# One written-out order exchanged for another: chunk-selecting attention followed by a gated feed-forward layer

## The chip, the cores and the metric

The kernel runs on one core of one Trainium2 chip. The core has five engines, each with its own queue of instructions: TensorE (PE in the profile) for matrix products, VectorE (DVE), ScalarE (ACT), GpSimd (POOL), and SyncE (SP), which issues most transfers; GpSimd issues those of the weights, because they are cast from fp32 to fp16 on the way. The metric is the time of one execution on the device in microseconds (us), lower is better.

## The reference

```
k_min, k_max = per chunk of 32 keys, over the chunk                # 24 chunks
ub     = sum_d max(q * k_min, q * k_max)        # bound of a query on each chunk
top    = the 6 chunks with the highest bound, among those not in the future
attn   = softmax(q k^T / 8, only keys of these chunks, only keys not later)
x      = (attn v), heads side by side           # 3072 tokens x 512
out    = (sigmoid(x w_gate) * (x w_val)) w_out  # 512 -> 1536 -> 512
```

There are 4 batches, 8 heads, 768 positions and 64 values per head. Inputs and output are fp32; inside the kernel most products run on fp16.

## The kernel before

The 24 blocks of 128 tokens are put into units of three, u0 to u7 (`units`). u0 holds the first blocks of batches 0 to 2, in which no chunk has to be chosen (`first`); the first block of batch 3 goes into u2. For each other unit the keys and queries are turned (`kT`, `qT` on TensorE for u1 and u2, `kt`, `qf` on VectorE for the rest), the bounds are multiplied out (`ub`), VectorE finds the sixth highest per query (`ubn`, `mx`, `ap`, `apt`), and the chosen mask becomes 64 more rows of the queries (`hqm`), so that one product gives masked scores (`sc`). ScalarE takes the exponential (`exp`), GpSimd cuts the diagonal blocks (`cm`), TensorE multiplies with v (`pv`), VectorE divides (`rz`, `x`), and the result is turned into `xT`: on TensorE for the first units (`xps`), by a transposing transfer on SyncE's queue from u3 on. The feed-forward layer of a unit is 12 pieces of `g` and `v` products, ScalarE's `tanh`, VectorE's `hg`, and the output: `o` products for u0 to u3, and for u4 to u7 a scheme with seven products in place of eight (`pair`, with sums `sw`, `tw`; `by7` does the same to most gate products of u5 to u7, with sums `ss`, `tt`). Thirty products without use, `fl_0` to `fl_29`, stand near the start.

No scheduler decides anything when the kernel is built. The string `ORDER` lists all 2010 operations by name, each with its engine (P, A, V, G, S for TensorE, ScalarE, VectorE, GpSimd, SyncE), and `SLOTS` gives each buffer its place in its pool, such as one of the eight PSUM banks. `Plan.order` checks that every operation stands behind those that it depends on, and the operations are emitted in that sequence; so each engine's queue is the list cut down to its letter, and an engine waits at the first operation that is not ready. Each operation also carries a cost and a mark `port`, which `Plan.order` does not read. The list was made elsewhere, by a search that used such costs and marks.

The lines that matter below: L569 `fl`, L575 `ident16` (the fp16 identity, a cast of the fp32 one), L588 to L596 the weight transfers (`wgp` is a quarter of the first third of the gate weights, `wg0` the other three quarters, `wg1`, `wg2`, `wv0` to `wv2`, `wo0` to `wo2` are thirds), L614 to L645 the other loads, L687 `kfT`/`qfT`, L724 `scf`, L731 `cmf`, L738 `pvf`, L434 GpSimd's copies (`hkp...` writes a constant pattern into the keys' mask rows, `vc` casts v), L1237 `g` and `v`, L989 `x`, L994 the transposing transfer.

Of the kernel before, what the change touches and what calls it, by code (L numbers as in the profile page):

```python
# [111 lines left out]
hq0_u1_0=A tanh_u0_2=A tanh_u0_1=A hg_u0_1=V ubn1_u1=V v_u0_3=P tanh_u0_3=A hg_u0_3=V ubm1_u1=V hg_u0_2=V tanh_u0_0=A hg_u0_0=V
hk0_u1_0=A hq1_u1_1=A sc_u1_0_2=P exp_u1_0_2=A sc_u1_1_2=P sc_u1_0_1=P sc_u1_0_0=P exp_u1_1_2=A sc_u1_1_0=P sc_u1_1_1=P
exp_u1_0_0=A exp_u1_0_1=A v_u0_7=P wo0=G hqm0_u1_2=G sc_u1_2_2=P exp_u1_2_2=A sc_u1_2_0=P exp_u1_2_0=A sc_u1_3_0=P sc_u1_3_2=P
exp_u1_3_2=A exp_u1_1_0=A sc_u1_3_1=P exp_u1_3_1=A exp_u1_3_0=A v16_0_3=G wo1=G v_u0_4=P sc_u1_2_1=P v_u0_6=P exp_u1_2_1=A
hk1_u1_0=G v16_0_2=G wo2=G mx1_u1=V ap1_u1=V apt1_u1=V hqm1_u1_0=V g_u0_5=P tanh_u0_5=A v_u0_5=P exp_u1_1_1=A hqm1_u1_2=A g_u0_6=P
tanh_u0_6=A g_u0_7=P tanh_u0_7=A hg_u0_7=V v16_0_1=G cm_u1_3=G pv_u1_3=P cm_u1_2=G hk1_u1_1=G g_u0_4=P tanh_u0_4=A hg_u0_4=V
vf1_3=G hq1_u1_2=G pv_u1_2=P sc_u1_5_1=P sc_u1_4_2=P sc_u1_4_1=P rz_u1_1=V x_u1_1=V exp_u1_4_1=A v_u0_9=P v_u0_10=P xps_u1_1=P
xT_u1_1=A exp_u1_4_2=A hg_u0_6=V hk1_u1_3=V hg_u0_5=V v_u0_8=P g_u0_10=P tanh_u0_10=A kcr1=V hg_u0_10=V g_u0_8=P tanh_u0_8=A
hg_u0_8=V sc_u1_5_2=P exp_u1_5_2=A g_u0_9=P tanh_u0_9=A hg_u0_9=V sc_u1_4_0=P exp_u1_4_0=A cm_u1_1=G pv_u1_1=P cm_u1_0=G qn_u2_2=G  # L120
sc_u1_5_0=P pv_u1_0=P exp_u1_5_0=A sc_u1_6_1=P exp_u1_6_1=A sc_u1_6_2=P exp_u1_6_2=A exp_u1_5_1=A sc_u1_7_2=P sc_u1_7_0=P
g_u0_11=P qT_u2_2=P sc_u1_7_1=P tanh_u0_11=A exp_u1_7_2=A exp_u1_7_0=A exp_u1_7_1=A kn_u2_1=V kT_u2_1=P rz_u1_0=V x_u1_0=V
xps_u1_0=P cm_u1_5=G pv_u1_5=P cm_u1_4=G pv_u1_4=P qf_u2_2=V q1_u2=S qn_u2_1=V qT_u2_1=P sc_u1_6_0=P kt_u2_1=A exp_u1_6_0=A
# [139 lines left out]
c22_u67=V out_u67_b1=S p4_u67=P p4z_u67=P c21_u67=V out_u67_1=S  # L263
# [1161 lines left out]
```

## Time and profile before

| | us |
|---|---|
| median of 3 runs | 282.62 |
| lowest, highest | 282.24, 283.18 |
| the profiled execution | 283.43 |
| its span, from the first to the last instruction | 281.7 |
| TensorE busy in the span | 268.8 |
| VectorE, ScalarE, GpSimd busy | 235.7, 180.5, 163.3 |

The span is what the views of the profile divide up; the profiled execution took 1.73 us more than its span. A busy TensorE need not be at its peak, since a product that starts late is still counted as running until its modelled end. The granted clock of TensorE was 1.00 over the whole span.

### The profile page before, as it was taken

Reading aid. Unit: us, or ns where it says so; the run is one execution under the profiler, and the core shown is the slowest. Engines: PE = TensorE matmul, PEld = TensorE weight load, DVE = VectorE, ACT = ScalarE, POOL = GpSimd, SP = SyncE. Lnnn points to the kernel's source line nnn. Section 1 sums busy time; section 2 is a strip of 40 time slices with the busy share of each in tenths; the row PEclk is TensorE's granted clock in tenths of the full one; section 3 lists DMA queues with packets and bytes.
Section 4 is the critical chain, followed back from the end, with each engine's and each line's share of the span. In section 5 each row is a group of like instructions: output and inputs, shape, how many; then the busy total and the mean of one; then the engine's idle time right before and its main releaser. Section 6 shows DMA issues by size and latency. Waiting matters only on the chain.

```text
span 281.7 us, 7507 instructions
## 1 busy us (share of the span) xinstructions
PE 268.8 (95%) x2806; PEld 188.9 (67%) x2806; DVE 235.7 (84%) x686; ACT 180.5 (64%) x386; POOL 163.3 (58%) x262
## 2 busy tenths in 40 slices
PE   5868989999999999999999999999999999999994
PEld 4645657667855665556687657776888688778683
DVE  4889846697998998886999987977889998888885
ACT  6377868669957943559689979987983422341520
POOL 5797743638464781823869956842685568063450
PEclk9999999999999999999999999999999999999999
DMA  6999999899999598977897230100310033000304
GB/s 161 246 254 204 205 216 209 180 192 210 178 214 182 131 195 162 199 142 141 164 154 111 63 89 16 40 0 2 73 74 2 1 81 126 2 1 2 150 2 150
DMA packets 131717, 34.70 MB, mean 123 GB/s; under 512 B 119776, under 2 KB 128736, under 8 KB 131680
## 3 DMA queue, kind: packets, MB, share of 16 engines
q1 hardware_dynamic: 126912, 29.50, 50.2%
q0 software_dynamic: 4768, 4.72, 10.0%
q8 instruction: 22, 0.36, 0.6%
q14 instruction: 15, 0.12, 0.1%
HBM read 30.67 MB, written 6.29 MB: 131 GB/s over the span
## 4 chain that ended last, share of the span: by engine, by line
PE 81%; DMA 9%; DVE 6%; issue 1%; SPq 1%; POOL 0%; DVEq 0%; POOLq 0%
PE v_u L1237 19%; PE g_u L1237 14%; PE o_u L1286 11%; PE sc_u L935 11%; PE p_u L1060 10%; PE pv_u L968 6%; DMA wg<-in_moe_w_gate_dram 6%; PE p_g_u L1169 5%; PE ube_u L874 3%; DMA kq_u<-in_k_dram 2%; DMA kf<-in_k_dram 1%; DVE x_u L989 1%; DVE tw L1031 1%; DVE ox L1077 1%; DVE hg_u L1258 1%
## 5 line engine op out<-in xcount | busy, mean ns | idle before, releaser
L946 ACT ACTIVATE att_u<-sc_u 128x512 f16<-128x512 f32 (+3 forms) x184 | 86.8, 571 | 8.6 <-PE sc_u L935 7.3
L1237 PE MATMUL v_u<-xT_u,wv 128*128 128x384 f16 x384 | 72.4, 326 | 0.1
L1258 DVE SCALAR_TENSOR_TENSOR hg_u<-gate_u,v_u 128x384 f16<-128x384 f16 x96 | 51.0, 544 | 18.6 <-ACT gate_u L1249 9.3
L1249 ACT ACTIVATE gate_u<-g_u 128x384 f16<-128x384 f32 x72 | 35.2, 498 | 42.2 <-PE g_u L1237 36.9
L1237 PE MATMUL g_u<-xT_u,wg 128*128 128x384 f16 x288 | 56.0, 326 | 2.1 <-DMA wg<-in_moe_w_gate_dram 1.5
L952 POOL TENSOR_SCALAR_AFFINE_SELECT att_u<-att_u 128x384 f16<-128x384 f16 (+1 forms) x56 | 28.5, 517 | 40.9 <-ACT att_u L946 39.8
L1237 PEld LDWEIGHTS <-wv 128*128 128x128 f16 x384 | 36.1, 98 | 20.5 <-DMA wv<-in_moe_w_val_dram 0.4
L1237 PEld LDWEIGHTS <-wg 128*128 128x128 f16 x288 | 26.7, 98 | 19.5 <-DMA wg<-in_moe_w_gate_dram 3.0
L1286 PE MATMUL o_u<-wo,hg_u 128*128 128x512 f16 x144 | 34.3, 379 | 0.0
L968 PE MATMUL pv_u<-v,att_u 128*128 128x65 f16 x640 | 26.3, 193 | 0.0
L968 PEld LDWEIGHTS <-att_u 128*128 128x128 f16 x640 | 24.2, 98 | 2.9 <-issue 0.6
L1206 DVE TENSOR_TENSOR f_g_u<-p_g_u,f_g_u 128x192 f32<-128x192 f32 (+1 forms) x72 | 24.9, 384 | 1.0 <-PE p_g_u L1169 0.4
L935 PE MATMUL sc_u<-hqe,hke 128*128 128x128 f16 (+2 forms) x220 | 25.4, 243 | 0.2
L935 PE MATMUL sc_u<-hqo,hko 128*128 128x128 f16 (+2 forms) x220 | 24.1, 243 | 0.1
L1286 PEld LDWEIGHTS <-hg_u 128*128 128x128 f16 x144 | 13.7, 98 | 13.4
L935 PEld LDWEIGHTS <-hke 128*128 128x128 f16 x220 | 16.5, 98 | 5.3 <-issue 0.8
L935 PEld LDWEIGHTS <-hko 128*128 128x128 f16 x220 | 16.4, 98 | 4.7 <-issue 0.4
L651 POOL CAST v<-v 128x512 f16<-128x512 f32 x23 | 14.5, 633 | 3.0 <-DMA v<-in_v_dram 2.5
L1249 ACT ACTIVATE gate_u<-f_g_u 128x384 f16<-128x384 f32 x24 | 11.9, 519 | 5.6 <-DVE hg_u L1258 2.9
L989 DVE TENSOR_TENSOR x_u<-pv_u,rz_u 128x384 f16<-128x384 f32 (+1 forms) x28 | 14.6, 524 | 0.9 <-DMA xT_u<-x_u 0.5
L897 DVE MAX8 mx_u<-ubn_u 128x8 f32<-128x8 f32 (+16 forms) x152 | 12.7, 159 | 0.3
L841 DVE STREAM_TRANSPOSE qf_u<-q 128x384 f32<-128x384 f32 (+2 forms) x28 | 11.7, 437 | 1.2 <-DMA q<-in_q_dram 1.2
(187 smaller groups left out, 507.9 us busy)
## 6 DMA issues: line engine op xcount, KB each, us to landing
v<-in_v_dram SPq DMA_DIRECT2D x23, 256.0 KB, 4.7
k<-in_k_dram SPq DMA_DIRECT2D x12, 384.0 KB, 5.5
q<-in_q_dram SPq DMA_DIRECT2D x12, 384.0 KB, 5.5
out_dram<-osb_u SPq DMA_DIRECT2D x12, 256.0 KB, 3.4
out_dram<-sw SPq DMA_DIRECT2D x8, 256.0 KB, 2.1
wv<-in_moe_w_val_dram POOLq DMA_DIRECT2D x3, 512.0 KB, 10.2
wo<-in_moe_w_out_dram POOLq DMA_DIRECT2D x3, 512.0 KB, 18.9
qf<-in_q_dram SPq DMA_DIRECT2D x8, 128.0 KB, 3.4
```

The source lines that it names most:

```text
L651: plan.add(f"v16_{b}_{ib}", {POOL: pool(H * D)}, lambda e: nc.gpsimd.tensor_copy(v16[b % 2][:, ib, :, 0:D], at(t)), reads=[t], writes=[("v ...
L935: nc.tensor.matmul(at(t)[:, o:o + 128 * m], hk[b % 2][e_][:, p, 128 * jb:128 * jb + 128], hq[u.side][e_][:, p, 128 * x:128 * (x + m)], sta ...
L946: plan.add(f"exp_{u.name}_{h}_{y}", {ACT: act(n)}, lambda e, t=t, att=att, b0=b0, n=n: nc.scalar.activation(at(att)[:, b0:b0 + n], at(t), ...
L952: nc.gpsimd.affine_select(out=dv, in_=dv, compare_op=ALU.is_ge, fill=0.0, base=0, pattern=[[0, u.m], [1, 128]], channel_multiplier=-1)
L968: nc.tensor.matmul(at(pv)[:, last, x, :], at(att)[:, c:c + 128], v16[b % 2][:, jb, h, :], start=(jb == 0), stop=(jb == ib))
L989: plan.add(f"x_{u.name}_{p}", {DVE: dve(u.t)}, lambda e: nc.vector.tensor_tensor(at(x_).rearrange("p a (e d) -> p e a d", e=2), at(pv)[:, ...
L1060: nc.tensor.matmul(at(to)[:, side], a(j)[:, i], b(j)[:, i], start=j == i == 0, stop=j == 2 and i == 1)
L1206: plan.add(f"{p}_{name}", {POOL: pool2(192 * n), DVE: dve(192 * n)} if slow else {DVE: dve(192 * n)}, lambda e: both(e).tensor_tensor(dst( ...
L1237: nc.tensor.matmul(at(t), w16[:, c, 128 * fb:128 * fb + 128], at(u.xt)[:, c, :], start=(c == 0), stop=(c == 3))
L1249: plan.add(f"tanh_{u.name}_{fb}", {ACT: act(T, not seven[0])}, lambda e, gv=gv, gate=gate: nc.scalar.activation(at(gate), gv(), AF.Tanh, s ...
L1258: plan.add(f"hg_{u.name}_{fb}", {DVE: dve(T)}, lambda e, vv=vv, gate=gate, hg=hg, fb=fb: nc.vector.scalar_tensor_tensor(at(hg)[:, fb % 2], ...
L1286: nc.tensor.matmul(at(o), at(hgs[fc // 2])[:, fc % 2, 128 * tb:128 * tb + 128], wo16[:, fc, lo:hi], start=(fc == 0), stop=(fc == NFB - 1))
```

## The change

`ORDER` and `SLOTS` are replaced as a whole. The operations are the same 2010, with the same sizes; 701 stand on TensorE and 128 on SyncE in both. Of the rest 118 stand on another engine than before: VectorE has 526 in place of 540, ScalarE 398 in place of 385, GpSimd 257 in place of 256. The only other changed line gives the cast `ident16` the mark `port`, which nothing in the kernel reads.

The diff, cut to the one line and the head of the list:

```diff
 ORDER = """
-ident=G ones16=V fl_4=P fl_2=P fl_8=P fl_3=P fl_1=P fl_0=P fl_29=P k2_u1=S kn_u1_2=A qf1_0=S kf1_0=S kf0_0=S fl_6=P fl_5=P epat0=V
-ap0=V epat=G hkp110=A hkp000=A hkp001=V kT_u1_2=P kcr0=V kt_u1_2=V hk0_u1_2=G vf1_1=G hkp011=V hkp010=G vf1_2=G hkp100=G kf1_2=S
-kf0_1=S kfT_0=P kxf1=V fl_17=P fl_10=P fl_7=P kx0_u1_2=V ident16=V kf16_0=V qf0_0=S qfT_0=P qf16_0=V qf1_1=S kf1_1=S kfT_1=P
...
+vf1_1=G k2_u1=S qf0_0=S ones16=V fl_4=P v10=G epat0=V epat=G ident=G hkp000=G ident16=V hkp110=V kf0_0=S kf1_0=S fl_13=P fl_0=P
+fl_10=P fl_6=P fl_7=P fl_1=P fl_2=P fl_11=P fl_5=P fl_3=P kn_u1_2=A fl_8=P kT_u1_2=P kt_u1_2=A fl_9=P ap0=V kcr0=V kfT_0=P kxf1=V
+kxf0=V fl_17=P fl_12=P qf1_0=S qfT_0=P qf0_1=S qf1_1=S qfT_1=P kf1_1=S kf16_0=V hk1_u1_2=A hkp011=A fl_18=P qf16_0=A qf16_1=A
...
     const("ident16", {DVE: (150, 230)}, lambda e: nc.vector.tensor_copy(ident16, ident32),
-          reads=["ident32"], writes=["ident16"], prio=-1.0)
+          reads=["ident32"], writes=["ident16"], prio=-1.0, port=True)
```

Cut down to single engines, the head of the list reads (B before, A after):

```
POOL B: ident epat hk0_u1_2 vf1_1 hkp010 vf1_2 hkp100 v10 v16_0_0 cmf_0_0 cmf_0_1 wgp cmf_1_0 vc_1 cmf_1_1
        hkf0 wg0 wv0 cmf_2_0 vc_2 kn_u1_3 cmf_2_1 kn_u1_1 v11 wv1 wg1 hq0_u1_3 hk0_u1_3 hq1_u1_3 wv2 hk0_u1_1 wg2
POOL A: vf1_1 v10 epat ident hkp000 hkp010 hkp001 v16_0_0 cmf_0_0 cmf_0_1 hkp100 vf1_2 cmf_1_0 vc_1 cmf_1_1
        wg0 cmf_2_0 wgp wv0 cmf_2_1 qn_u1_0 wv1 qn_u1_2 wg1 qm_u1_3 wv2 kcr_f hkf1 hkp101 wg2
DVE  B: ones16 epat0 ap0 hkp001 kcr0 kt_u1_2 hkp011 kxf1 kx0_u1_2 ident16 kf16_0 qf16_0 kf16_1 hq0 ap1 qf16_1
DVE  A: ones16 epat0 ident16 hkp110 ap0 kcr0 kxf1 kxf0 kf16_0 kf16_1 rzf_0_0 xf_0_0 rzf_0_1 xf_0_1 qf16_2
ACT  B: kn_u1_2 hkp110 hkp000 expf_0_1 expf_0_0 expf_1_0 expf_1_1 hk1_u1_2 kf16_2 expf_2_1 expf_2_0
ACT  A: kn_u1_2 kt_u1_2 hk1_u1_2 hkp011 qf16_0 qf16_1 expf_0_0 expf_0_1 expf_1_1 expf_1_0 hkp111 kn_u1_0 kf16_2
SP   B: k2_u1 qf1_0 kf1_0 kf0_0 kf1_2 kf0_1 qf0_0 qf1_1 kf1_1 qf0_1 vf_0 qf0_2 qf1_2 kf0_2 vf_1 k0_u1 q3_u1 q2_u1
        vf_2 q1_u1 k3_u1 q0_u1 k1_u1 v_0_3 v_0_2 v_0_1 qf1_3 k0_u2 q2_u2 k1_u2 q1_u2 q3_u2 q0_u2 k2_u2 k3_u2 qf0_3
SP   A: k2_u1 qf0_0 kf0_0 kf1_0 qf1_0 qf0_1 qf1_1 kf1_1 vf_0 kf0_1 qf0_2 qf1_2 k0_u1 q0_u1 kf0_2 kf1_2 vf_1 q3_u1
        q1_u1 vf_2 k3_u1 q2_u1 k1_u1 v_0_3 v_0_2 v_0_1 q2_u2 q1_u2 k1_u2 k0_u2 q3_u2 q0_u2 k2_u2 k3_u2 qf1_3
```

On TensorE the same operations stand ahead of the first `g` product in both lists (all thirty `fl`, the turns of the first blocks and of u1). Between that product and the first one on the last third of the gate weights (`g_u0_10`) the new list has three operations more: `sc_u1_5_2`, `sc_u1_5_0` and `pv_u1_0`. Of the turns of batch 3's first block `kfT_3` now stands behind 133 operations of TensorE in place of 135, and `qfT_3` behind 134 in place of 132; `o2_u0_1` stood ahead of `kfT_3` and now follows it. In SyncE's queue `xT_u5_3`, which completes u5's input, stood behind `xT_u6_1`, `xT_u6_2` and `xT_u6_0`, and now stands behind the first two of them. Further on the sequence of every stage is another, and ends in the same way: the seven products of the last output block, each behind its sums, with `p4_u67` and `out_u67_1` last.

More of the change, by code (lines that the diff above doesn't have):

```diff
@@ L352 @@
+gate_u7_6:1 v_u7_6:5 hg_u7_3:1 gate_u7_7:0 v_u7_7:1 p1_g4_u7:1 f0_g4_u7:2 f1_g4_u7:1 p26_g4_u7:1 p53_g4_u7:6 p74_g4_u7:7
+gate_u7_8:1 v_u7_8:0 hg_u7_4:4 gate_u7_9:0 v_u7_9:5 g_u7_10:7 gate_u7_10:3 v_u7_10:3 hg_u7_5:6 g_u7_11:6 gate_u7_11:2 v_u7_11:4
+p1_u7:1 p26_u7:6 p5_u7:7 p3_u7:4 p7_u7:0 p4_u7:2 p1_u67:3 p26_u67:3 p5_u67:5 p3_u67:1 p7_u67:6 p4_u67:7
 """
```

495 lines of the change are left out of this document (246 added, 249 removed).

## The prediction

> **What bounds the kernel now.** I read the page first, then the chain of waits in order of time, then what each engine waited for, then the first 45 us engine by engine.
>
> ```profile
> span 281.7 us, 7507 instructions
> PE 268.8 (95%) x2806; PEld 188.9 (67%) x2806; DVE 235.7 (84%) x686; ACT 180.5 (64%) x386; POOL 163.3 (58%) x262
> PE   5868989999999999999999999999999999999994
> DMA  6999999899999598977897230100310033000304
> PE 81%; DMA 9%; DVE 6%; issue 1%; SPq 1%; POOL 0%; DVEq 0%; POOLq 0%
> ```
>
> TensorE bounds it: dense from the third slice (7 us each) to the last. The transfers are as full over the first eight slices, so until some 57 us the data's arrival sets a floor of its own. The chain says where TensorE did not set the pace.
>
> ```profile
> 5.81 1.10 PE kfT L687 x4
> 13.20 6.11 DMA kq_u<-in_k_dram
> 27.00 15.51 DMA wg<-in_moe_w_gate_dram
> 42.57 1.47 PE g_u L1237 x8
> 176.17 0.56 DVE x_u L989
> 176.73 0.95 DVE mx_u L897 x12
> 178.32 0.87 issue
> 180.01 0.57 DVE x_u L989
> 186.91 0.77 DVE tw L1031
> 189.93 0.57 DVE x_u L989
> 277.85 0.70 DVE ox L1077
> ```
>
> The last third of the gate weights, issued at 27.00, held TensorE until 42.57. Between 43 and 277 us the longer pieces that are not TensorE's sum to 0.56 + 0.95 + 0.87 + 0.57 + 0.77 + 0.57 = 4.3 us; that is about all that any order could still win there. The end is one VectorE pass and a store.
>
> ```profile
> PE pvf L738 <- POOL vh L434: 1.9, 2, 1.2
> PE g_u L1237 <- DMA wg<-in_moe_w_gate_dram: 1.5, 2, 1.3
> PE g_u L1237 <- ACT xT_u L430: 0.6, 1, 0.6
> ```
>
> These columns are us in total, times, and the longest. All lie in the first 45 us. What happens there, engine by engine:
>
> ```profile
> 1.07 0.29 POOL masks.py:199 TENSOR_SCALAR_AFFINE_SELECT ident<-ident 128x128 f32<-128x128 f32 x1
> 4.00 0.55 DVE L432 COPY hke<-epat 64x1536 f16<-64x1536 f16 x1 [1.74 <-POOL epat L544]
> 5.34 0.54 DVE L432 COPY hko<-epat 64x1536 f16<-64x1536 f16 x1
> 5.57 0.67 POOL L434 COPY hke<-kt_u 64x384 f16<-64x384 f16 x1 [1.60 <-DVE kt_u L432]
> 7.82 1.46 POOL L434 COPY hke<-epat 64x1536 f16<-64x1536 f16 x1
> 8.00 1.36 DVE L575 CAST ident<-ident 128x128 f16<-128x128 f32 x1
> 9.29 0.68 DVE L432 CAST kf<-kfT 128x512 f16<-128x512 f32 x1
> 10.61 0.40 PE L724 MATMUL scf<-qf,kf 64*128 64x128 f16 x8 [0.76 <-DVE qf L432]
> 13.38 0.79 POOL L588 DMA_DIRECT2D wg<-in_moe_w_gate_dram  x1
> 16.46 0.80 POOL L590 DMA_DIRECT2D wg<-in_moe_w_gate_dram  x1
> 23.65 0.32 PE L1237 MATMUL g_u<-xT_u,wg 128*128 128x384 f16 x1 [0.59 <-ACT xT_u L430]
> 24.23 1.31 PE L1237 MATMUL g_u<-xT_u,wg 128*128 128x384 f16 x7 [0.26 <-DMA wg<-in_moe_w_gate_dram]
> 37.15 0.43 PE L968 MATMUL pv_u<-v,att_u 128*128 128x65 f16 x9
> 37.43 0.81 PE L1237 MATMUL g_u<-xT_u,wg 128*128 128x384 f16 x4
> 42.57 1.47 PE L1237 MATMUL g_u<-xT_u,wg 128*128 128x384 f16 x8 [1.27 <-DMA wg<-in_moe_w_gate_dram]
> 44.64 0.39 PE L935 MATMUL sc_u<-hqo,hko 128*128 128x128 f16 x4
> 44.86 0.44 PE L968 MATMUL pv_u<-v,att_u 128*128 128x65 f16 x9
> ```
>
> The cast at 8.00 ended at 9.36, just after GpSimd's copy (7.82 to 9.28): it sat behind that copy. The other way round at 5.34: VectorE's copy was first and took its 0.54, and GpSimd's of 5.57 took 0.67, with 0.31 of it beside the other. The first feed-forward product ran its first quarter at 23.65 and went on at 24.23, when the rest of its weights had come. The times to landing are on the page:
>
> ```profile
> wg<-in_moe_w_gate_dram POOLq DMA_DIRECT2D x1, 384.0 KB, 7.7
> wg<-in_moe_w_gate_dram POOLq DMA_DIRECT2D x1, 128.0 KB, 5.8
> ```
>
> So the small piece issued at 13.38 was there at 19.2, and the large one, issued at 16.46, at 24.2.
>
> **The change part by part.** The mark `port` emits nothing: 0. TensorE's work is the same, and its clock was full, so only the time in which it is held up can change.
>
> *Engines.* VectorE loses 14 operations, at 235.7/686 = 0.34 us some 4.8 us; ScalarE gains 13, at 180.5/386 = 0.47 us some 6.1; GpSimd gains one, 0.6. None bounds the whole (TensorE has 268.8), so I count 0, covered by TensorE's queue. Where that cover is thin, in the 176 to 190 us of the chain, VectorE's relief can give back up to the 4.3 us above, and ScalarE's load can cost as much.
>
> *The identity, the patterns and the first scores.* GpSimd now makes the pattern before the identity, and then three pattern copies (1.46 each) in a row. The cast moves from tenth to third on VectorE, straight behind the identity, with a pattern copy behind it. The pattern was done at 3.97 (the copy at 4.00 waited for it); the identity's two small steps, which ended at 1.36 after a start near 0.8, put it at 4.6. If nothing hinders them, cast and copy end by 5.4, and the two reductions and the cast of the first keys, 0.68 each, follow kfT's end at 6.9: 8.95. If the cast loses one GpSimd copy (to 6.1) and then both run, the copy ends at 6.8; with two fills at an estimated 0.3 each and three times 0.68 that is 9.4. If the copy loses a second one (to 7.5), it is 10.7. Before, that cast of keys ended at 9.97, and the scores began at 10.61 with the queries' cast, which is ScalarE's now and early. I take 9.5 for the first scores, 1.1 earlier, by the nearest row, that of 8.00: one copy lost (bounds 9.1 and 10.8). The Trainium skill, "SBUF — State Buffer", section "SBUF: two separate sides", tells of such a pair: VectorE in its two-port modes and GpSimd share one pair of ports, as a lock that the first comer holds for a whole instruction. By that rule the second copy may be lost too, and my sum would be 0.2 higher, through the 10.7; the rows of 5.34, 5.57 and 8.00 agree with the rule, and no row shows who wins when GpSimd's next copy is ready.
>
> *The gate weights.* Before, the small piece went out at 13.38, ahead of the large one; now it goes behind the large one and behind one more mask, that of the third block, whose keys are loaded later than before. The large one still stands behind the second block's masks, and gains the 1.1: 15.4. The small one I put at 18.4, two of GpSimd's issues (0.80) behind the old place of the large one. What the small one took of the transfers between 13.4 and 19.2 it now takes at the end of that line: a third of the large one's 7.7 is 2.6 at most; 0 if the earlier start makes room. I take 0.4, nearer to 0, since before 24.2 the same bytes come in either order. The first product needs the small piece, so it starts in earnest at 24.23 + 0.4 = 24.6 (24.2 to 26.8).
>
> *The wait at 42.57.* Two score banks (0.22 from 44.64 to 44.86 for the larger, half of it for the other) and one product with v (0.28, from 37.15 to 37.43) are put ahead of it: 0.6 us. When the last third lands is set by the bytes ahead of it, so I leave it at 42.5 (0.8 earlier at best, one GpSimd issue). TensorE's queue reached it at 42.57 - 1.27 = 41.3; now at 41.3 + 0.4 + 0.6 = 42.3. Some 0.2 of the wait is left, and behind it 0.6 more is done than before: gain 0.6. Bounds for this part and the last together: gain 1.3 if the third lands at 41.7, loss 1.3 if the start is 2.6 late (2.6 less the wait of 1.27).
>
> *The loads behind.* Batch 3's first keys come after the same bytes as before, and TensorE asks for them earlier by what it has gained and by an output product that now follows them: I take back 0.3 of the 0.6 (0 to 0.6).
>
> *The middle, 57 to 270 us.* Every stage is reordered. The distances in the list between a product, its reader on another engine and the next use are about as long as before; in SyncE's queue the transfer that completes u5's input has one transposing transfer less ahead of it and about 1 us less of TensorE's work between. None of it is seen in this trace, so I bound it: -4.3 (all other engines' pieces go) to +4.3 (as many new ones come). I take +0.4: nearer to zero than to either end since the distances are alike, and on the losing side since the old pieces are few to begin with.
>
> *The end.* The last block's seven products stand behind the same sums, and the 0.70 of VectorE and the store stay: 0 (-0.3 to +0.5).
>
> Sum: 0 + 0 - 0.6 + 0.3 + 0.4 + 0 = +0.1 on the profiled 283.43 (span 281.7 and 1.73 around it). That execution lay 0.81 above the median of the runs, so I forecast 282.62 + 0.1 = 282.7.
>
> **The rivals.** *Faster.* The first product starts at 24.2, the last third lands at 41.7, and the whole wait of 1.27 goes; 0.3 is given back at the loads, and VectorE's 4.8 us less takes an eighth of the 4.3 in the middle, 0.5: 282.62 - 1.5 = 281.1. For it: VectorE stands in five of the six pieces of the middle, and the scores start earlier. Against: the transfers' line is full in this stretch.
>
> *Slower: the small weight piece holds the start.* One place, GpSimd's queue at the issue that now follows the third block's mask. If it lands at 26.8, the 2.6 exceed the old wait by 1.3, and with the 0.4 of the middle it is 282.62 + 1.7 = 284.3; nothing is then lost at the loads. It decides from a landing after 25.9, where the loss passes 0.45 and with the 0.4 the 0.85. For it: the third block's keys are now the fifteenth and sixteenth load instead of the fifth and fourteenth, and TensorE waited 1.9 us for GpSimd's cast of v in this stretch already. Against: the large piece starts earlier.
>
> *Slower: new holes in the middle*, 1.5 us of the 4.3 and more: 282.62 - 0.3 + 1.7 = 284.0. For it: ScalarE has 6.1 us more, and the transfer for u5 has less work in front of its user. Against: the distances are as long as before.
>
> *The change does not do what it says:* the cast still takes 1.4 beside a copy. My sum holds that already, at no price.
>
> **How the numbers follow.** Within 0.3% (0.85 us, about what a measurement of this kernel tells from no change) I put 0.36, at 282.7; faster, 0.30, at 281.1; slower, 0.34, half of it each rival's, near 284.2. The range reaches past both sides, 280.9 to 285.0, and leaves about one in ten beyond each end. The forecast's own is 281.8 to 283.5.
>
> **What would show it.** Right: the cast L575 again above 1 us, first scores between 9 and 10, the first product in earnest after 24.4, a wait of at most 0.5 for the gate weights at 42, pieces that are not TensorE's in the chain after 57 us of 4 to 5 us, the same last pass and store. Wrong: the small weight piece issued after 19 or landing after 25.9 (slower), the last third landing before 42 (faster), or new waits in rows of L1060, L1169 or L935.

## The result and the profile after

| | before | after |
|---|---|---|
| median, us | 282.61 (6 runs) | 285.92 (6 runs) |
| lowest, highest | 282.24, 284.05 | 284.79, 288.21 |
| the profiled execution | 283.43 | 285.42 |
| its span | 281.7 | 283.7 |

The change makes the kernel slower by about 1.2%: after/before is 1.0119, with a 95% interval of 1.0072 to 1.0165. A second measurement, in the experiments, gave 1.0140 (1.0116 to 1.0164). The forecast of 282.7 and its range up to 285.0 both miss it.

The page of the changed kernel, the lines that answer to those shown of before (busy time and share by engine, two rows of tenths by slice, and the chain by engine):

```profile
span 283.7 us, 7525 instructions
PE 271.3 (96%) x2806; PEld 190.5 (67%) x2806; DVE 234.6 (83%) x672; ACT 189.1 (67%) x399; POOL 170.3 (60%) x263
PE   7968999999999999999999999899999999999995
PEclk9988999999999999999999999999999999999999
PE 76%; DVE 9%; DMA 9%; issue 2%; POOL 2%; SPq 0%; ACT 0%; DVEq 0%; POOLq 0%; ACTq 0%
```

TensorE is still what bounds it, but two things are new: an 8 among the 9s of its row late in the span, and two 8s in its clock. In the chain, pieces on VectorE went from 6 to 9%. What TensorE waited for between 57 and 277 us, by the view of waits (us in total, times, longest); the same view of before, over the same stretch, has no row at all:

```profile
PE sc_u L935 <- DVE hg_u L1258: 1.1, 2, 0.9
PE p_u L1060 <- DVE sw L1077: 0.6, 1, 0.6
PE sc_u L935 <- DVE sw L1085: 0.5, 1, 0.5
PE v_u L1237 <- DVE hg_u L1258: 0.3, 1, 0.3
```

Every row names a VectorE operation that reads a PSUM bank (`hg`, and those of lines 1077 and 1085, which add up products `p`), and on TensorE a product that does not need its result. What the product needs is the bank: it is the next owner. So the view shows holes, places where TensorE stood still because VectorE had not yet emptied a bank. TensorE's busy time over the stretch gives the size, first of before, then of after:

```profile
57.00:277.00 220.00, 219.70 (x2359) 155.74 (x2358) 193.28 (x565) 141.81 (x302) 126.67 (x194) 1.00 0.49 99
```

```profile
57.00:277.00 220.00, 217.20 (x2331) 152.80 (x2308) 192.00 (x551) 147.89 (x312) 128.27 (x194) 1.00 0.49 98
```

Idle went from 0.30 to 2.80 us, at a clock of 1.00 in both. The modelled end of a product overlaps the next product's start by 0.16 us when nothing waits, so I count a hole as the idle time of a row plus 0.16; a row that reads 0.54 is a hole of 0.70. So counted, and from 0.12 us upwards, before has three holes (0.23, 0.26, 0.30; together 0.79) and after has eight (0.28 at 61 us, 0.46 at 134, 0.40 and 0.13 at 180, 1.05 at 183, 0.70 at 201, 0.81 at 209, 0.22 at 274; together 4.05). Those at 61 and 274 us wait for an operand that VectorE makes, all others for a bank. The difference, 3.26 us, is the whole of the 3.3 that the medians show. (The spans of the two profiled executions lie only 2.0 apart, since the changed one had come to the middle a microsecond sooner; the account of the prediction below says why that lead counts for little.)

Two names are needed for what follows: `tw` (L1031) are sums of parts of the output weights, `sw` (L1047) sums of hidden values, both made for the later units, where seven products `p` of such sums give an output block. The largest hole, in the view by time (start, duration, engine, line, output and inputs; in brackets the idle time before it and what ended it). These are VectorE, GpSimd and TensorE around 183 us of the changed kernel:

```profile
181.65 1.37 DVE L1031 TENSOR_TENSOR tw<-wo 128x512 f16<-128x512 f16 x1
182.94 0.77 DVE L902 TENSOR_TENSOR ap<-ubn_u,mx_u 128x288 f16<-128x288 f32 x1
183.64 0.54 DVE L1258 SCALAR_TENSOR_TENSOR hg_u<-gate_u,v_u 128x384 f16<-128x384 f16 x1
...
181.56 1.18 POOL L1031 TENSOR_TENSOR tw<-wo 128x512 f16<-128x512 f16 x1
...
181.44 0.81 PE L1237 MATMUL v_u<-xT_u,wv 128*128 128x384 f16 x4
...
184.23 0.32 PE L935 MATMUL sc_u<-hqo,hko 128*128 128x384 f16 x1 [0.89 <-DVE hg_u L1258]
```

The product `v_u4_3` was done at 182.25. Its reader `hg_u4_3` started only at 183.64, behind a weight sum `tw0_1` and a threshold step `ap0_u7`, and the scores that wanted the bank started 0.05 after it ended. The weight sum took 1.37 us; GpSimd's weight sum `tw0_0` had started 0.09 before it and ended 0.28 before it. The hole at 201 us:

```profile
199.90 1.21 POOL L1031 TENSOR_TENSOR tw<-wo 128x512 f16<-128x512 f16 x1
...
200.11 1.14 DVE L1047 TENSOR_TENSOR sw<-hg_u,hg_u 128x256 f16<-128x256 f16 x1
201.28 0.29 DVE L1047 TENSOR_TENSOR sw<-sw,hg_u 128x256 f16<-128x256 f16 x1
201.49 0.42 DVE L1085 TENSOR_SCALAR sw<-p_u 128x256 f32<-128x256 f32 x1
...
201.96 0.79 PE L935 MATMUL sc_u<-hqo,hko 128*128 128x128 f16 x7 [0.54 <-DVE sw L1085]
```

Again a sum on VectorE (`sw0_u4_1`) takes 1.14 us beside a weight sum of GpSimd (`tw2_2`), where its like just below it takes 0.29; behind both stands `p1s_u4` of line 1085, which empties the bank. The hole of 0.40 at 180 us has the same look (`ap1_u7` beside `tw2_1`, with `hg_u4_2` behind it):

```profile
177.83 1.36 DVE L902 TENSOR_TENSOR ap<-ubn_u,mx_u 128x288 f16<-128x288 f32 x1
...
177.72 1.16 POOL L1031 TENSOR_TENSOR tw<-wo 128x512 f16<-128x512 f16 x1
```

At 134 us the reader `hg_u3_1` stands behind `hk1_2_2`, a copy that the change took from ScalarE to VectorE:

```profile
133.00 0.88 DVE L432 COPY hko<-kt 64x768 f16<-64x768 f16 x1
133.91 0.55 DVE L1258 SCALAR_TENSOR_TENSOR hg_u<-gate_u,v_u 128x384 f16<-128x384 f16 x1
...
132.63 1.03 POOL L434 CAST k<-k 128x768 f16<-128x768 f32 x1
```

The copy takes 0.88 beside GpSimd's cast of keys, and 0.40 in the first experiment below, where it comes later. The step ahead of it, `qm_u5_0`, takes 1.18 beside another of GpSimd's casts, where another of the same size takes 0.55. No run moved these casts, so how much of this hole comes from the stretching is not shown.

The hole at 209 us has another cause, SyncE's queue:

```profile
202.40 4.43 SPq L994 DMA_TRANSPOSE xT_u<-x_u  x3
...
207.12 0.58 DVE L1031 TENSOR_TENSOR tw<-wo,tw 128x512 f16<-128x512 f16 x1
208.65 0.66 DVE L1149 TENSOR_TENSOR hqe<-xT_u 128x384 f16<-128x384 f16 x1 [0.95 <-DMA xT_u<-x_u]
209.23 1.21 DVE L1077 SCALAR_TENSOR_TENSOR sw<-p_u,sw 128x256 f32<-128x256 f32 x2
...
209.70 0.49 PE L1060 MATMUL p_u<-tw,hg_u 128*128 128x256 f16 x3 [0.65 <-DVE sw L1077]
```

Three transposing transfers follow each other on SyncE from 202.40, when the first, `xT_u5_3`, got its data. The third, `xT_u6_0`, whose data had been ready since 188 us, landed at 208.6. VectorE waited 0.95 for it in front of `tt0_u6` (L1149), and `c12_u4` (L1077), which empties a bank, was queued behind that.

The stretch up to 57 us went much as it had been reckoned:

```profile
4.64 0.23 DVE L575 CAST ident<-ident 128x128 f16<-128x128 f32 x1 [2.78 <-POOL ident masks.py:199]
4.78 1.82 DVE L432 COPY hko<-epat 64x1536 f16<-64x1536 f16 x1
...
9.12 0.56 PE L724 MATMUL scf<-qf,kf 64*128 64x128 f16 x8
...
24.44 0.99 PE L1237 MATMUL g_u<-xT_u,wg 128*128 128x384 f16 x5 [1.33 <-DMA wg<-in_moe_w_gate_dram]
...
42.34 0.82 PE L1237 MATMUL g_u<-xT_u,wg 128*128 128x384 f16 x4 [0.30 <-DMA wg<-in_moe_w_gate_dram]
```

One thing in it had not been thought of, TensorE's clock. Three stretches (their bounds, their length, TensorE's busy time, the granted clock, and the share and GB/s of the transfers):

```profile
16.40:19.70 3.30, 1.59 (x20) 1.00 1.11 260
19.80:23.10 3.30, 3.30 (x19) 0.50 1.19 198
23.20:26.60 3.40, 2.16 (x32) 1.00 1.22 197
```

TensorE ran at half its clock for 3.4 us, behind a stretch of the same length in which it was busy for 48%. That made a rival to the holes: perhaps the lost clock is the loss.

### The profile page after: what moved, and what is told of

Its sections match the earlier page's. It is cut to its first block, busy times and chain, and to the rows that moved or that the text cites. A ratio compares the mean times of both kernels' runs of the same rounds, so it can differ in the third digit from the quotient of the medians.

```text
span 283.7 us, 7525 instructions
## 1 busy us (share of the span) xinstructions
PE 271.3 (96%) x2806; PEld 190.5 (67%) x2806; DVE 234.6 (83%) x672; ACT 189.1 (67%) x399; POOL 170.3 (60%) x263
## 4 chain that ended last, share of the span: by engine, by line
PE 76%; DVE 9%; DMA 9%; issue 2%; POOL 2%; SPq 0%; ACT 0%; DVEq 0%; POOLq 0%; ACTq 0%
PE v_u L1237 18%; PE g_u L1237 13%; PE o_u L1286 10%; PE sc_u L935 9%; PE p_u L1060 7%; DMA wg<-in_moe_w_gate_dram 6%; PE pv_u L968 5%; PE p_g_u L1169 5%; PE ube_u L874 3%; DVE sw L1047 2%; DVE hg_u L1258 2%; DMA kq_u<-in_k_dram 2%; DMA xT_u<-x_u 1%; PE qfT L687 1%; POOL epat L544 1%
## 5 line engine op out<-in xcount | busy, mean ns | idle before, releaser
L946 ACT ACTIVATE att_u<-sc_u 128x512 f16<-128x512 f32 (+3 forms) x184 | 85.6, 558 | 11.5 <-PE sc_u L935 10.5
L952 POOL TENSOR_SCALAR_AFFINE_SELECT att_u<-att_u 128x384 f16<-128x384 f16 (+1 forms) x56 | 29.2, 530 | 31.8 <-ACT att_u L946 29.9
L1237 PEld LDWEIGHTS <-wg 128*128 128x128 f16 x288 | 26.5, 98 | 18.4 <-DMA wg<-in_moe_w_gate_dram 2.4
L968 PE MATMUL pv_u<-v,att_u 128*128 128x65 f16 x640 | 27.3, 193 | 0.0
L968 PEld LDWEIGHTS <-att_u 128*128 128x128 f16 x640 | 25.0, 98 | 2.9 <-issue 0.6
L935 PE MATMUL sc_u<-hqo,hko 128*128 128x128 f16 (+2 forms) x220 | 24.7, 243 | 1.5 <-DVE hg_u L1258 0.9
L935 PE MATMUL sc_u<-hqe,hke 128*128 128x128 f16 (+2 forms) x220 | 24.1, 243 | 0.2 <-DVE hg_u L1258 0.2
L1077 DVE SCALAR_TENSOR_TENSOR sw<-p_u,sw 128x256 f32<-128x256 f32 (+1 forms) x20 | 10.6, 529 | 2.3 <-PE p_u L1060 1.2
```

The source lines that it names most:

```text
L935: nc.tensor.matmul(at(t)[:, o:o + 128 * m], hk[b % 2][e_][:, p, 128 * jb:128 * jb + 128], hq[u.side][e_][:, p, 128 * x:128 * (x + m)], sta ...
L946: plan.add(f"exp_{u.name}_{h}_{y}", {ACT: act(n)}, lambda e, t=t, att=att, b0=b0, n=n: nc.scalar.activation(at(att)[:, b0:b0 + n], at(t), ...
L952: nc.gpsimd.affine_select(out=dv, in_=dv, compare_op=ALU.is_ge, fill=0.0, base=0, pattern=[[0, u.m], [1, 128]], channel_multiplier=-1)
L968: nc.tensor.matmul(at(pv)[:, last, x, :], at(att)[:, c:c + 128], v16[b % 2][:, jb, h, :], start=(jb == 0), stop=(jb == ib))
L1237: nc.tensor.matmul(at(t), w16[:, c, 128 * fb:128 * fb + 128], at(u.xt)[:, c, :], start=(c == 0), stop=(c == 3))
```

## Experiments

Three theories stand against each other. *Banks:* the time lost is the sum of the holes. *Clock:* it is the stretch at half clock. *Load:* the other engines simply carry more, and holes mended here come up there. Later a fourth question arose, why VectorE was late: the order of its list, or GpSimd's hold on a shared port. Intervals are those of 95%; kernels that are measured side by side ran on one chip.

### VectorE's list mended in four places

Cut down to VectorE, the changed list (-) and the experiment (+):

```diff
-hk1_2_2 hg_u3_1 ... tw0_1 ap0_u7 hg_u4_3 ... sw0_u4_1 sw1_u4_1 p1s_u4 ... tt0_u6 c12_u4
+hg_u3_1 hk1_2_2 ... hg_u4_3 tw0_1 ap0_u7 ... p1s_u4 sw0_u4_1 sw1_u4_1 ... c12_u4 tt0_u6
```

> The changed kernel with four places of VectorE's list mended and nothing else: hk1_2_2 behind hg_u3_1; tw0_1 and ap0_u7 behind hg_u4_3; sw0_u4_1 and sw1_u4_1 behind p1s_u4; tt0_u6 behind c12_u4. Each time the operation that empties a PSUM bank goes first. Bank theory: the four holes of TensorE (0.46 at 134, 1.05 at 183, 0.70 at 201, 0.81 at 209 us, together 3.0) shrink to 0.3 in all, so 285.9 - 2.7 = 283.2 us. Rival, the clock: TensorE's clock was half from 19.8 to 23.1 us in the changed kernel's trace, and that is the loss; then nothing changes, 285.9. Rival, the load: the other engines simply carry more (ScalarE 8.6, GpSimd 7.0 us more than before), so holes reappear next to the old places and at most half comes back, 284.5 or more.

Measured: 283.66 us, 1.0053 of before (1.0029 to 1.0077). The four holes went, and 1.74 us are left in all, with three new ones: 0.39 at 200 us (behind `x_u5_3`, which stands behind the two sums), 0.20 at 211 and 0.15 at 252. Over before on the same chip the time is now 1.3 us, where it was 3.3, and the holes fell by 2.3; about a quarter of what had been mended came up elsewhere. That is for the banks, and against the load.

### One transfer moved

```diff
-xT_u5_3 xT_u6_3 xT_u6_0        (SyncE)
+xT_u6_0 xT_u5_3 xT_u6_3
```

> The changed kernel with one exchange in SyncE's list and nothing else: the transposing transfer xT_u6_0, whose data is ready at 188.4 us, goes ahead of xT_u5_3, which waits until 202.4 for its own. Bank theory, with the transfers' queue as cause of the fourth hole: VectorE no longer waits 0.95 us for xT_u6_0 in front of tt0_u6, c12_u4 empties its bank early, and the hole of 0.81 at 209 us goes, the other three stay: 285.9 - 0.8 = 285.1. If the queue is not the cause (VectorE is late anyway), the hole stays and the time is 285.9.

Measured: 284.89 us, 1.0096 (1.0058 to 1.0133). The hole at 209 us is gone, the other seven stand at the same operations with the same sizes: 3.21 in all. So the fourth hole was made by the transfers' queue.

### Before, spoilt in four places

```diff
-hg_u3_1 qf0_u6_2 osb_u2_1 k16_3_0 ... hg_u4_3 hg_u4_5 ... p1s_u4 x_u5_3 x_u6_3 ... c12_u4 m1_g1_u5 tw3_1 held_u4_3
+qf0_u6_2 osb_u2_1 k16_3_0 hg_u3_1 ... hg_u4_5 hg_u4_3 ... x_u5_3 x_u6_3 p1s_u4 ... m1_g1_u5 tw3_1 held_u4_3 c12_u4
```

> The kernel before with four operations of VectorE's list put behind later ones, and nothing else: hg_u3_1 behind k16_3_0, hg_u4_3 behind hg_u4_5, p1s_u4 behind x_u6_3, c12_u4 behind held_u4_3. Bank theory: the next owner of each bank then starts late by 0.4 (sc_u4_0_0, at 134 us), 0.45 (sc_u7_7_2, 185), 1.5 (sc_u7_5_2, 200) and 0.65 (sc_u7_0_1, 207), so 282.6 + 3.0 = 285.6 us, with no operation moved to another engine. Load theory: the engines carry what they carried, 282.6 to 283.2. Clock theory: 282.6.

Measured: 285.1 us, 1.0103 (1.0066 to 1.0139), against 285.6 expected. The view of waits, 57 to 277 us:

```profile
PE sc_u L935 <- DVE sw L1085: 1.3, 1, 1.3
PE sc_u L935 <- DVE hg_u L1258: 0.7, 2, 0.4
PE sc_u L935 <- DVE sw L1077: 0.2, 1, 0.2
```

Four holes of 0.54, 1.44, 0.47 and 0.38 stand where they were expected, no operation having changed its engine. Four displaced readers of banks cost before about what the whole change does.

### The clock, first attempt

```diff
-    for i in range(30):
+    for i in range(56):
         keep_awake(i)
...
-... xpsf_1_0 pvf_2_0 ... xpsf_1_1 qT_u1_3 ... qT_u1_2 g_u0_0
+... xpsf_1_0 (6 fl) pvf_2_0 ... xpsf_1_1 (8 fl) qT_u1_3 ... qT_u1_2 (12 fl) g_u0_0
```

> The changed kernel with 26 more filler products on TensorE, which compute nothing that is used: 6 in the gap at 16.8 us, 8 in the gap at 17.9, and 12 behind the last transposition at 23 us. Both theories expect the granted clock to stay at 1.00 from 19.8 to 23.1 us, where it was 0.50. Clock theory: the 1.3 us of lead that the changed kernel lost between 20 and 26 us come back to the end, 284.6. Bank theory: the first feed-forward product starts when its last weights land (24.39) with either clock, so the time stays at 285.9, give or take 0.3.

Measured: 290.11 us, 1.0288 (1.0250 to 1.0326), and in the profiled execution the clock did not stay up (its mean was 0.982, though 1.000 in three of the six executions). Both theories missed, because the fillers did not do what I thought (TensorE by time; then one of its stretches as above):

```profile
26.70 4.09 PE L569 MATMUL fl<-ones 128*128 128x256 f16 x12
```

```profile
30.40:33.70 3.30, 3.23 (x17) 0.50 1.20 214
```

The twelve fillers ahead of the first feed-forward product took 4.09 us: all were put into one PSUM bank, and there they start 0.33 us apart, where three fillers from 10.24 us on, spread over banks, start 0.11 apart. They stood in the way of `g_u0_0` and held it until 30.84. So this run cannot tell the theories apart; the next pair can.

### All that could be mended, without and with a full clock

```diff
 # the four places and the exchange of the transfers as above, and
-hq1_u2_1 hqm1_u2_0 ... ap1_u7 hg_u4_2 ... sw0_u4_1 sw1_u4_1 x_u5_3 ... sw2_u7_0 ... sw3_u7_0 ... sw1_u7_2
+hqm1_u2_0 hq1_u2_1 ... hg_u4_2 ap1_u7 ... x_u5_3 sw0_u4_1 sw1_u4_1 ... sw1_u7_2 sw2_u7_0 sw3_u7_0
 # second kernel, on TensorE, each group spread over banks that are free there
+... fl_22 (5 fl) ... xpsf_1_0 (6 fl) ... xpsf_1_1 (8 fl) ... qT_u1_2 (12 fl) g_u0_0
```

> The four mended places of the changed kernel's lists, the exchange of the two transposing transfers, and four more places of VectorE's list: hqm1_u2_0 ahead of hq1_u2_1 (hole of 0.28 at 61 us), hg_u4_2 ahead of ap1_u7 (0.40 at 180), x_u5_3 ahead of sw0_u4_1 (0.39 at 200 in the kernel with the four places mended), and sw2_u7_0 and sw3_u7_0 behind sw1_u7_2 (0.22 at 274). Bank theory: these 1.3 us come on top of the 2.3 that the four places gave, 283.66 - 1.2 = 282.5 us, level with the kernel before, and TensorE's holes between 57 and 277 us sum to under 0.5. If the limit has moved to VectorE's total work, new holes appear behind the moved operations and the time stays at 283.3 or more.

> The same with 31 more filler products, whose results are not used, in TensorE's four gaps between 14 and 24 us, this time spread over banks that are free there, so that each takes 0.11 us and not 0.33. It is to be set beside the kernel without them on the same chip. Clock theory (each stretch of 3.4 us at half clock in the head costs about 1 us, as the runs of single kernels with mean clocks of 1.00, 0.99 and 0.98 suggest): the mean clock is 0.998 or more in nearly all runs, and the median falls by 1.0, to 281.5 us. Bank theory alone (the head waits for its weights whatever the clock): the time stays within 0.3 of the kernel without them.

Measured: 283.10 us without fillers, level with before (0.9992, 0.9966 to 1.0018), and 283.15 with them (1.0015, 0.9998 to 1.0032). Each kernel was measured in 12 runs. Without fillers the mean granted clock was 0.986 to 0.994 in 11 of them; with fillers it was 0.998 to 1.000 in all 12. The stretches of the kernel with fillers:

```profile
16.40:19.70 3.30, 3.12 (x32) 1.00 1.06 246
19.80:23.10 3.30, 2.71 (x29) 1.00 1.13 189
```

The clock is held, and the time does not move, where the clock theory had forecast 1.0 us. In both traces the first feed-forward product starts when its last weights have landed: at 24.76 us without fillers, after 1.58 of waiting, and at 24.95 with them, after 0.48. (In the changed kernel TensorE waited 1.33 us at 24.44, right behind its stretch at half clock.) That the fillers cost something of their own, which a full clock gives back, this pair does not exclude. In each of the two kernels 1.09 us of holes are left, where under 0.5 had been expected: 0.21 and 0.25 at 64 and 65 us, to which mending the one at 61 moved it, 0.26 at 182, 0.15 at 253, and 0.22 at 273, which its mending did not touch.

### The identity's cast alone

```diff
-epat0 ident16 hkp110 ap0 kcr0 kxf1 kxf0 kf16_0 kf16_1        (VectorE)
+epat0 hkp110 ap0 kcr0 kxf1 kxf0 kf16_0 ident16 kf16_1
```

> The changed kernel with one move on VectorE: the fp16 identity's cast goes from third place to behind the cast kf16_0 of the first keys, about where it stood before the change, beside a pattern copy of GpSimd. If a cast on VectorE waits for GpSimd's port, it takes over 1 us there again, as in the kernel before (1.36), where it took 0.23 in third place; the pattern copy of VectorE, which took 1.82 us behind the cast, keeps that time, since it is GpSimd's copy that holds it. If the place has nothing to do with it, the cast takes 0.2 to 0.3 us. The end moves by less than the spread of the runs, since the first weights land at 24 us either way.

Measured, one execution: 286.10 us. Neither expectation holds (VectorE by time):

```profile
2.95 0.55 DVE L432 COPY hko<-epat 64x1536 f16<-64x1536 f16 x1 [1.10 <-POOL epat L544]
...
8.85 0.75 DVE L575 CAST ident<-ident 128x128 f16<-128x128 f32 x1
```

The cast takes 0.75 beside GpSimd's copy, between the 0.23 that it took where nothing ran beside it and the 1.36 of before. The pattern copy now runs at 2.95, as soon as its part of the pattern is made, and takes 0.55; in the changed kernel it had stood behind the cast, which waited for the identity, and so met GpSimd's own copy and took 1.82. The keys' cast starts at 8.25 instead of 8.34; one execution shows no move of the end (the changed kernel's medians are 285.92 and 286.47).

### GpSimd's weight sums moved, VectorE's list untouched

The mended lists show that the order is a cure, not that it is the cause. In three of the places a VectorE operation had been stretched beside a weight sum of GpSimd. The change had brought these there. Line 1031 on GpSimd, before and after (durations in ns, least, median, greatest; first and last start):

```profile
L1031 POOL TENSOR_TENSOR tw<-wo x1: 1152/1152/1152, 177.9 to 177.9; 128x512 f16<-128x512 f16 x1
```

```profile
L1031 DVE TENSOR_TENSOR tw<-wo x3: 411/420/1370, 167.1 to 193.6; 128x512 f16<-128x512 f16 x3
L1031 POOL TENSOR_TENSOR tw<-wo x3: 1156/1182/1206, 177.7 to 199.9; 128x512 f16<-128x512 f16 x3
```

Of the 12 weight sums GpSimd had one and now has three. The first experiment moved all three to other places of GpSimd's list:

```diff
-cm_u6_5 tw2_1 hq1_u7_2 cm_u6_1 tw0_0 cm_u6_0 cm_u5_7 ss1_g1 ... cm_u7_7 cm_u7_1 ss2_g1 tw2_2        (GpSimd)
+cm_u6_5 hq1_u7_2 cm_u6_1 cm_u6_0 cm_u5_7 ss1_g1 tw0_0 ... cm_u7_7 tw2_2 tw2_1 cm_u7_1 ss2_g1
```

> The changed kernel with three moves in GpSimd's list and none in VectorE's: tw2_2 and tw2_1 go behind cm_u7_7 (where GpSimd is idle from 194.4 us), tw0_0 behind ss1_g1. These three ran beside VectorE's sw0_u4_1 (1.14 us there, 0.28 where nothing ran beside it), ap1_u7 (1.36 against 0.75) and tw0_1 (1.37 against 0.67). Lock theory: VectorE's operations in front of the late bank-emptying ones are late because GpSimd holds the shared port; then the holes at 180 (0.40) and 201 us (0.70) go and that at 183 falls from 1.05 to 0.5, 1.65 us together, without any change of VectorE's order: 285.9 - 1.65 = 284.3. List theory: the order in VectorE's list alone makes the holes, and they stay as they are, 285.9.

Measured: 285.01 us, 1.0088 (1.0068 to 1.0109). In the trace the holes at 180, 183 and 201 us are gone, with VectorE's order untouched; one of 0.62 came at 186, where the moved `tw0_0` now runs beside VectorE's `tw1_1`, which takes 1.27 us. That makes 2.38 us of holes. It is the sum that was expected, but by luck: 2.28 went in place of 1.65, and the 0.62 had not been foreseen. The time fell by less than the holes did: 2.55 over before on that chip, where the holes give 1.6. The profiled execution, at 283.42, was the fastest of its 12, so its trace does not show what the others lost; this rest of 1 us stayed open. The second kernel leaves `tw0_0` where it was, beside the changed kernel itself on one chip:

```diff
-cm_u6_5 tw2_1 hq1_u7_2 ... cm_u7_7 cm_u7_1 ss2_g1 tw2_2        (GpSimd)
+cm_u6_5 hq1_u7_2 ... cm_u7_7 tw2_2 tw2_1 cm_u7_1 ss2_g1
```

> The changed kernel with two moves in GpSimd's list and none in VectorE's: tw2_2 and tw2_1 go behind cm_u7_7, and tw0_0 stays where the change put it (moved, it stretched tw1_1 to 1.27 us and made a hole of 0.62 at 186 us). Lock theory: ap1_u7 takes 0.5 to 0.75 us instead of 1.36 and sw0_u4_1 0.28 instead of 1.14; VectorE then reaches tw0_1 before GpSimd reaches tw0_0, so that the holes at 180, 183 and 201 us (0.40, 1.05, 0.70) all go, with 0.3 left at most, and those at 61, 134, 209 and 274 (1.8 together) stay: 1.9 to 2.2 us less than the changed kernel on the same chip. If the time of this kernel is not the sum of its holes, as 285.01 instead of 284.05 in the last such run could mean, it ends within 1.2 us of the changed kernel.

> The changed kernel itself, for its time beside the one above on the same chip and for a second trace of it. Bank theory: the same holes at the same operations (0.28, 0.46, 0.40, 1.05, 0.70, 0.81, 0.22, give or take 0.1), 1.0 to 1.2 per cent above the kernel before. If the holes were chance of one execution, they stand elsewhere.

Measured: 283.29 us with the two moves (1.0046, 1.0026 to 1.0066), 286.47 for the changed kernel (1.0140, 1.0116 to 1.0164): the places of two operations on an engine that is idle for 40% of the time are worth 3.2 us (1.9 to 2.2 had been expected), 2.3 of them in the holes of the traces; where the rest of 0.9 lies is not shown. The holes of the changed kernel's second trace are those of the first, to 0.03 us each, so they belong to the lists and not to one execution. VectorE of the kernel with two moves, by time, and below it what TensorE still waits for:

```profile
177.60 0.45 DVE L902 TENSOR_TENSOR ap<-ubn_u,mx_u 128x288 f16<-128x288 f32 x1
177.97 0.55 DVE L1258 SCALAR_TENSOR_TENSOR hg_u<-gate_u,v_u 128x384 f16<-128x384 f16 x1
...
180.43 0.42 DVE L1031 TENSOR_TENSOR tw<-wo 128x512 f16<-128x512 f16 x1
...
198.51 0.24 DVE L1047 TENSOR_TENSOR sw<-hg_u,hg_u 128x256 f16<-128x256 f16 x1
```

```profile
PE p_u L1060 <- DVE sw L1077: 0.6, 1, 0.6
PE v_u L1237 <- DVE hg_u L1258: 0.3, 1, 0.3
```

The same three operations take 0.45, 0.42 and 0.24 us where they took 1.36, 1.37 and 1.14. So the holes at 180, 183 and 201 us, 2.15 of the 4.05, come from GpSimd's hold on the port; the order of VectorE's list matters only because these operations stood ahead of the ones that empty banks. The Trainium skill, "SBUF — State Buffer", section "SBUF: two separate sides", says that the pair of ports which VectorE and GpSimd share is locked for a whole instruction by whoever starts first, and that a VectorE operation with two inputs in SBUF takes part in this. The rows agree: each of the three began 0.09 to 0.21 us after GpSimd's and ended 0.15 to 0.31 us after it, so that it did most of its work only when the other was done.

### The changed kernel with its causes removed, and before improved

```diff
 # the changed kernel, GpSimd
-cm_u6_5 tw2_1 hq1_u7_2 ... cm_u7_7 cm_u7_1 ss2_g1 tw2_2
+cm_u6_5 hq1_u7_2 ... cm_u7_7 tw2_2 tw2_1 cm_u7_1 ss2_g1
 # the changed kernel, VectorE and SyncE
-hk1_2_2 hg_u3_1 ... xT_u5_3 xT_u6_3 xT_u6_0
+hg_u3_1 hk1_2_2 ... xT_u6_0 xT_u5_3 xT_u6_3
 # the kernel before, VectorE
-ap1_u7 hg_u4_2 rz_u6_2 x_u6_2 ... tw1_1 ss0_g4 rz_u6_0 x_u6_0
+hg_u4_2 rz_u6_2 x_u6_2 ap1_u7 ... rz_u6_0 x_u6_0 tw1_1 ss0_g4
```

> The changed kernel with four moves in its lists: GpSimd's tw2_2 and tw2_1 behind cm_u7_7 as in the last study, VectorE's hk1_2_2 behind hg_u3_1, and SyncE's xT_u6_0 ahead of xT_u5_3. Bank and lock theory: of the changed kernel's 4.0 us of holes between 57 and 277 us only those at 61 (0.28) and 274 (0.22) are left, 0.5 against the 0.8 of the kernel before; if the head is worth nothing, the time is that of the kernel before less 0.3, and if the head's forecast gain of 0.3 were real, less 0.6: 281.7 to 282.2 us where before has 282.4. If the change loses something besides these holes, it stays above before by that.

> The kernel before with three places of VectorE's list mended: hg_u4_2, rz_u6_2 and x_u6_2 ahead of ap1_u7 (holes of 0.23 and 0.26 at 180 us), rz_u6_0 and x_u6_0 ahead of tw1_1 and ss0_g4 (0.30 at 190.5). Bank theory: the 0.8 us of holes that the kernel before has between 57 and 277 us fall to about 0.1, and it ends 0.7 sooner, 281.9 us where before has 282.6, the fastest of all. If its time is not set by these holes (the head or the transfers set it), it stays at 282.6.

Measured: the changed kernel with four moves 282.01 us, level with before (0.9990, 0.9962 to 1.0019), 0.49 of holes left; before improved 281.61, 0.9961 of before (0.9935 to 0.9987), no hole left between 57 and 277 us. The second beats both kernels: the three holes of before were worth the 0.8 us that they measured.

The kernels side by side, in us. The holes stand less the 0.79 of before, the time less the median of before on the same chip:

| kernel | holes | time |
|---|---|---|
| after | +3.26 | +3.3, again +4.2 |
| one transfer moved | +2.42 | +2.5 |
| four places mended | +0.95 | +1.3 |
| three weight sums moved | +1.59 | +2.6 |
| two weight sums moved | +0.98 | +1.0 |
| all mended | +0.30 | +0.4 |
| all mended, full clock | +0.30 | +0.4 |
| four moves | -0.30 | +0.1 |
| before spoilt | +2.53 | +2.8 |
| before improved | -0.79 | -0.9 |

With the changed head, the stretch up to 57 us, the time lies above the holes in all nine measurements, by under 0.5 us in seven of them and by 1.0 in two; with the head of before it lies 0.2 above and 0.1 below. So that stretch gained nothing, and may have lost a few tenths. One part of the change was never exchanged alone: `SLOTS`, which decides what product owns a bank next. All mending was done in the lists, with the new slots in place, so what the slots add to the holes stays open.

## Why the prediction was wrong

*The middle, 57 to 270 us.* This is the step that failed: +0.4 forecast, 3.3 measured. The sentence behind it, that "the distances in the list between a product, its reader on another engine and the next use are about as long as before", looked at the wrong thing. What counted was when the reader could run, and that was set by what stood ahead of it on VectorE and by how long that took. The bound of +4.3 held, but it had been read off the old pieces and was no mechanism. Nor were those 4.3 us to be won: TensorE itself stood still for 0.79 us there before, and mending that gave 0.85.

*Engines at 0.* "None bounds the whole (TensorE has 268.8), so I count 0" was a count of operations by engine means, and both halves failed. VectorE lost 14 operations and 1.1 us, not 4.8; GpSimd gained one operation and 7.0 us, not 0.6; ScalarE gained 8.6, not 6.1. Which operations moved was left out; by name it is 127 that changed their engine, not the 118 given with the change, and 35 of them went from VectorE to GpSimd against 25 the other way. Three weight sums of 1.16 to 1.21 us stand on GpSimd in place of one, and they made 2.15 us of holes, through the lock that the prediction had described, with its page, for the identity's cast alone. "Where that cover is thin, in the 176 to 190 us of the chain" named a stretch that holds 1.6 of the 4.05 us, but blamed ScalarE for it; no hole between 57 and 277 us was ended by ScalarE.

*The transfer for u5.* The one that "has one transposing transfer less ahead of it" pointed at the right place. The loss of 0.81 there came to the transfer that had been put behind it, `xT_u6_0`: a queue that waits in order makes late what is ready.

*The identity and the first scores.* The cast took 0.23, not over 1: it came before GpSimd's copy and won. VectorE's copy behind it lost to GpSimd's and took 1.82, so that it ended at 6.60, near the 6.8 of the sum. The first scores began at 9.12 against 9.5, inside the bounds, by another way; the cast moved alone changed nothing at the end.

*The gate weights and the wait at 42.57.* Start 24.44 against 24.6, with the small piece landing last (issued at 17.14 in place of 18.4, there at 24.39); wait of 0.30 left against 0.2, at 42.34 against 42.3: right for this execution. In seven of the other nine traces with the changed head no such wait was left. And the 0.6, and 0.3 after the loads, did not last beyond one execution. The last product of u2's bounds ended at 57.7 in the changed execution that was profiled first and at 58.7 in that of before, but between 57.0 and 59.2 us in ten traces with the changed head (median 58.0) and at 57.1, 57.8 and 58.7 in three with that of before. The landing of the weights moves by a microsecond either way between executions, and I had taken one of them for the rule.

*The clock.* "Its clock was full, so only the time in which it is held up can change" left out that a sparse head can halve it. It did halve, in some executions of before too; held at full by fillers, it gave nothing that the medians show. Three executions with a mean clock of 0.980 to 0.982 lay 1.1 to 3.2 us above the median of their kernel; whether the clock made them late, or what made them late took the clock, no run tells.

*The end.* Right: the chain ends in the same VectorE pass, 0.70 us at 279.81, and a store.

*The rivals.* "New holes in the middle" was the right mechanism, at half the size, and with ScalarE's load as a reason that played no part.

## What to carry to other kernels

In a kernel bound by TensorE, list for each PSUM bank its reader and the next owner, and look at what stands ahead of the reader on its engine; the slack of each such reader, not the load of the engine, prices a reordering. An operation that moves to GpSimd can be paid on VectorE as well, in those operations beside it that need the shared port (the three above took 0.24 to 0.45 us alone and 1.14 to 1.37 beside GpSimd's sums, while the readers `hg` took 0.50 to 0.56 in every trace), so long sums on GpSimd belong where VectorE waits anyway. A queue of transfers that waits in order should hold the ready ones first.

## What the hardware showed that was not expected

The clock of TensorE halved in whole stretches of 3.4 us (one, or two in a row), in some executions of every kernel without extra fillers; in their traces the stretch of that length ahead of it had been busy for 42 to 69%, not idle. The Trainium skill, "TensorE: Matmul & The Clock Gate", section "Part 1: The HAM clock gate", gives the same length and a window that runs free of the kernel's start, and the traces agree; that half clock comes after an idle window does not agree with 1.59 us busy in 3.30 ahead of the halved stretch above. With the fillers spread over banks, at 82 to 95% in the two rows shown, no execution of 12 lost its clock. Where they stood 0.33 us apart, a stretch that counts as 82% busy was followed by one at half clock, so the share alone does not give a threshold.

Products of 256 columns that follow each other in one bank started 0.33 us apart, for the most part at full clock, and 0.11 apart when spread over banks at full clock. Near the start even spread ones stand 0.21 to 0.22 apart: up to 8.77 us in the changed kernel and up to 7.11 in before, and then 0.11 from 10.11 and 11.50 on. In other traces 0.11 is there at 6 us, and before improved, the fastest kernel of all, still shows 0.21 at 11.75. So it seems that TensorE begins at half its pace, although the views print a clock of 1.00 there, and for before over the whole span; the mean clocks leave this stretch out. That it costs anything is not shown.

GpSimd's operations pay for the lock too: beside VectorE's threshold step the weight sum `tw0_0`, 1.18 us in the changed kernel, took 1.35 in the kernel with two moves, and its second pattern copy took 1.70 beside VectorE's, where the first and third took 1.52 and 1.46.
